# Expert stage of an attention and router kernel: TensorE order given by hand, x eviction ahead of the weight copies, four buffers for the second weight

## Chip, cores and metric

The kernel runs on one core of one Trainium2 chip. The metric is the device time of one launch in microseconds (us), the median of several runs; lower is better. In what follows PE is TensorE, PEld its weight loads, ACT is ScalarE, DVE is VectorE, POOL is GpSimd and SP is SyncE.

## What is computed

Attention with polynomial sketch features, and behind it a layer of eight experts. A router gives each of 4352 tokens (128 numbers each) to one expert, by the best cosine. All is float32. Cut to what matters here:

```python
x = attention_output.reshape(4352, 128)          # N tokens of D = 128
expert_idx = np.argmax(logits, axis=1)           # one of E = 8 experts for each token
for e in range(8):
    mask = expert_idx == e
    h = np.maximum(x[mask] @ w1[e], 0.0)         # w1[e]: 128 x 1024
    out[mask] = gate_w[mask, None] * (h @ w2[e]) # w2[e]: 1024 x 128
```

## The kernel before

The first part (up to about 110 us) computes the attention and the logits. Its instructions are recorded in ticks, and a scheduler sets their order on each engine. The tokens, scaled by their gates, are written to a DRAM buffer `x_dram`. Then `route_and_run_experts` sorts the tokens by expert and pads each expert's group to whole blocks of 128 tokens; 41 blocks always suffice (`NBLK`). One integer per block, `exp_i`, says whose expert's block it is.

The experts run one block at a time. Both weights of all experts lie in SBUF (`w1_sb`, `w2_sb`). For a block i there are these steps:

- `fetch(i)` (L494 on): POOL issues an indirect DMA that gathers the 128 tokens of the block from `x_dram` into `xs` (L497). Fetches are recorded four blocks ahead (`AHEAD`); `xs` has six buffers.
- `prepare(i)` (L501 to L512): DVE loads the expert's number into a register, copies that expert's first weight to `w1b` (L506) and the second to `w2b` (L507); both tags, `kp` and `a`, have two buffers, shared with the attention part. PE transposes `xs` into PSUM (L510), and DVE evicts the result to `xTb` (L512).
- `up(i)` (L514 to L522): eight matmuls in two halves of four (u = 0 and 1), each half into its own half of a PSUM tile `ps_big` of 2 x 512 columns (L521). Behind each half, ACT applies relu and writes that half of `hT` (L522). `ps_big` and `hT` have two buffers.
- `down(i)` (L524 to L533): eight matmuls add up into `ps_acc` (L528), ACT copies the sum to `y` (L530), and POOL issues an indirect DMA that scatters `y` to the rows of the output (L531).

In each pass of the loop the recording order is fetch of block i + 4, `up(i)`, `prepare(i + 1)`, `down(i - 1)`.

What sets the order on the engines: the whole of `route_and_run_experts` is recorded with `tc.manual_schedule` for DVE alone. So DVE runs its instructions as recorded, while PE, ACT, POOL and SP get theirs from the scheduler. The scheduler mixes the matmuls of neighbouring blocks: in the built program a typical stretch of PE is half 0 of up, three matmuls of down, a transpose, half 1 of up, one matmul of down, half 0 of the next up. Waits between engines are semaphores that the tile framework sets from the tiles that each instruction reads and writes; a wait holds up all that stands behind it on its engine.

Of the kernel before, what the change touches and what calls it, by code (L numbers as in the profile page):

```python
# [11 lines left out]
F32 = mybir.dt.float32  # L12
# [7 lines left out]
P = 128  # L20
B, H, S, D = 4, 4, 1088, 32
R = 8                   # rows of each sketch; R * R features per head
DM = H * D              # 128, the width of a token
N = B * S
E, F = 8, 1024
NF = F // P
HALF = P // 2           # partitions per batch: a tile of tokens is half of two batches
NC = S // HALF          # 17 tiles per pair of batches
NK = S // P             # 8 tiles of keys in each batch by itself, and a 17th of both's rest
SK = NK * P  # L30
NM = B // 2             # pairs of batches
NT = NM * NC            # 34 tiles of 128 tokens
NBLK = (N + E * (P - 1)) // P   # 41: the most blocks of 128 that 8 padded groups of N tokens can fill
K_GROUPS = ((0, 4), (4, 8), (8, 12), (12, 16), (16, 17))
# [3 lines left out]
PROB_EPS = 1e-9  # L38
NOWHERE = 8192.0        # added to a padding slot's destination row: past the output's end
DIGIT = 128             # tokens are counted in two digits  # L40
AHEAD = 4               # blocks whose tokens are fetched ahead of their arithmetic


def bview(t, free):
    """The tile t with the free dims given as [step, count] pairs."""
    return bass.AP(tensor=t.tensor, offset=t.offset, ap=[list(t.ap[0])] + [list(d) for d in free])
# [3 lines left out]
def kernel(  # L50
# [13 lines left out]
    nc = tc.nc  # L64
# [4 lines left out]
    rows_p = ctx.enter_context(tc.tile_pool(name="rows", bufs=4))  # L69
# [11 lines left out]

# [1 line left out]
    swords = consts.tile([2 * R, D, 2], U32, name="swords")  # L83
# [6 lines left out]
    def load_q(m):  # L90
        # token 2*S*m + NC*p + c is row p of tile (m, c)
        for i in range(2):
            for h in range(H):
                nc.sync.dma_start(  # L94
                    q_sb[m][i * HALF:(i + 1) * HALF, :, h],
                    bass.AP(tensor=q.tensor, offset=q.offset + ((2 * m + i) * H + h) * S * D,
                            ap=[[NC * D, HALF], [D, NC], [1, D]]))

    # tiles i * NK + j of keys and values: rows NK*p + j of batch 2*m + i; the last: the rest of both
    v_sb = [consts.tile([P, 6, NC, D], F32, name=f"v{m}") for m in range(NM)]  # L100

# [44 lines left out]

# [1 line left out]
    ident = consts.tile([P, P], F32, name="ident")  # L148
# [13 lines left out]

    # The sketches come as the words of float64 numbers. Float32's sign, exponent and high 23 bits of
    # the mantissa are the same bits, closer together; the low 29 are worth rem * 2**(exponent - 52).
    lo, hi = swords[:, :, 0], swords[:, :, 1]
# [24 lines left out]
    nc.vector.tensor_copy(ST, ps[:, :2 * R])  # L190
    # Sblk and enT are filled up to 96 columns with zeros: wide moving operands for the tensor engine
    Sblk = consts.tile([P, 6, 2 * R], F32, name="Sblk")
# [58 lines left out]

# [1 line left out]
    kz = {}  # L253
    acc = {}

    def k_steps(m, c0, c1):
        n = c1 - c0
        s = {}
# [21 lines left out]
        def kv():  # L280
            if c0 == 0:
                acc[m] = [ps_acc(i)[:, :6 * D].rearrange("p (a n) -> p a n", a=2) for i in range(2)]
            for c in range(c0, c1):
                rest = c == NC - 1
                for i in range(2) if rest else (c // NK,):
                    r = slice(i * HALF, (i + 1) * HALF) if rest else slice(0, P)
                    for p in range(2):
                        nc.tensor.matmul(  # L288
                            acc[m][i][:, p],
                            s["kp"][r, c - c0, 2 * p:2 * p + 2].rearrange("s h i j -> s (h i j)"),  # L290
                            v_sb[m][r, 3 * p:3 * p + 3, c],
                            start=c == i * NK and p == 0, stop=rest, skip_group_check=True)
            if c1 == NC:
                for i in range(2):
                    # per head: its D value columns, then the sum of its features
                    z = consts.tile([P, 2, 2, D + 1], F32, name=f"kz{2 * m + i}")
                    t = acc[m][i]
                    nc.vector.tensor_mul(z[:, :, :, :D], t[:, :, :2 * D].rearrange("p a (h d) -> p a h d", h=2),
                                         bview(maskh, [[0, 2], [1, 2], [0, D]]))
                    zs = t[:, :, 2 * D:2 * D + 1]  # L300
                    nc.vector.tensor_mul(z[:, :, :, D], bview(zs, [list(zs.ap[1]), [0, 2]]),
                                         bview(maskh, [[0, 2], [1, 2]]))
                    kz[2 * m + i] = z.rearrange("p a h d -> p a (h d)")
# [75 lines left out]
    def pick(m):  # L379
        """The first best expert of each token, one-hot."""  # L380
        l, o = lg[:, m], oh[:, m]
# [6 lines left out]
        nc.vector.reduce_max(out=mx[:], in_=t[:], axis=AX.X)  # L388
        # a token with no best one (not a number) goes to the first, as with argmax
        nc.vector.tensor_scalar(t[:, :, 0], mx, 0.0, float(E), op0=ALU.is_equal, op1=ALU.mult)  # L390
# [3 lines left out]
    def gate_tokens(m):  # L394
        """The tokens scaled by their gates and kept in DRAM by token: a positive factor of a token
        is one of its expert's output, which is made of products and relu."""
        l = lg[:, m]
# [15 lines left out]
    def route_and_run_experts():  # L413
# [1 line left out]
        pick(1)  # L415
# [34 lines left out]

        # token + 1 of each slot of each block, 0 where the slot is padding: sums of one product each,
        # of its two digits, which like the one-hot factors are whole in bfloat16
        ps_tok = ps_acc(0)[:, :2 * NBLK]
# [28 lines left out]

        # the expert of each block: how many experts end at or before it
        ends = consts.tile([1, NBLK, E], F32, name="ends")
# [6 lines left out]

# [1 line left out]
        xs, xT, wt, hT = {}, {}, {}, {}  # L493

# [5 lines left out]

        def prepare(i):  # L501
            e = nc.values_load(exp_i[0:1, i:i + 1], engines=(mybir.EngineType.DVE,), min_val=0, max_val=E - 1,
                               skip_runtime_bounds_check_because="a count of experts, clamped to the last one")
            a = work.tile([P, F], F32, tag="kp", name="w1b")
            b = work.tile([P, NF, DM], F32, tag="a", name="w2b")
            nc.vector.tensor_copy(a, w1_sb[:, bass.ds(e, 1)].rearrange("p o f -> p (o f)"))  # L506
            nc.vector.tensor_copy(b, w2_sb[:, bass.ds(e, 1)].rearrange("p o f d -> p (o f) d"))  # L507
            wt[i] = (a, b)
            ps = ps_small()
            nc.tensor.transpose(ps[:, :P], xs.pop(i), ident)  # L510
            xT[i] = work.tile([P, P], F32, tag="sq", name="xTb")
            nc.vector.tensor_copy(xT[i], ps[:, :P])  # L512

        def up(i):  # L514
            ps = ps_big()
            hT[i] = work.tile([P, 2, 512], F32, tag="qp", name="hT")
            x = xT.pop(i)
            for u in range(2):
                for j in range(4):
                    f = 4 * u + j  # L520
                    nc.tensor.matmul(ps[:, u, j * P:(j + 1) * P], wt[i][0][:, f * P:(f + 1) * P], x, start=True, stop=True)  # L521
                nc.scalar.activation(hT[i][:, u], ps[:, u], ACT.Relu)  # L522

        def down(i):  # L524
            ps = ps_acc(i % 2)[:, :DM]
            h, w = hT.pop(i).rearrange("p u n -> p (u n)"), wt.pop(i)[1]
            for f in range(NF):
# [5 lines left out]
                in_=y[:], in_offset=None, bounds_check=N - 1, oob_is_err=False)  # L533

        for i in range(AHEAD):
            fetch(i)
        prepare(0)
        for i in range(NBLK + 1):
            if i + AHEAD < NBLK:
                fetch(i + AHEAD)  # L540
            if i < NBLK:
                up(i)
            if i + 1 < NBLK:
                prepare(i + 1)
            if i > 0:
                down(i - 1)
# [24 lines left out]

    with tc.manual_schedule(engines={mybir.EngineType.DVE}):
        route_and_run_experts()
# [30 lines left out]
```

## Time and profile before

| | us |
|---|---|
| median of 3 runs | 317.56 |
| lowest and highest of them | 317.02, 320.74 |
| profiled execution: span from its first to its last instruction | 315.2 |
| busy in this span: PE, PEld | 261.8, 232.3 |
| busy in this span: DVE, ACT, POOL | 139.9, 93.2, 108.3 |
| mean granted clock of TensorE | 0.926 |
| from 147 to 303 us (156 us): PE, PEld busy | 155.6, 149.9 |
| from 147 to 303 us: DVE, ACT, POOL busy | 61.4, 57.7, 80.7 |

The profile shows one execution. Its own time beyond the span is not recorded on the page; the median of the runs is 2.4 us above the span. The page has one busy row for each engine over 40 equal slices of the span, a row of granted TensorE clock (9 means 90% or more of full speed), and groups of equal instructions with their busy time, the mean of one, and the idle time ahead of them with what ended it. The timeline lists the instructions of an engine in order, merged where equal ones follow each other; "x8" counts records, and a float32 matmul of 128 x 128 leaves two weight loads and two matmul records, a transpose one of each.

### The profile page before, as it was taken

How to read it: one execution, taken by the hardware profiler on the slowest of the kernel's cores; microseconds unless marked ns; L12 is line 12 of the kernel's file. 1: busy time of each engine (PE TensorE's matmuls, PEld its weight loads, DVE VectorE, ACT ScalarE, POOL GpSimd, SP SyncE). 2: the span in 40 equal slices, each digit the busy share in tenths (PEclk: the TensorE clock that was granted, in tenths of full speed). 3: DMA queues.
4: the chain of work that ended last, by engine and by line, in shares of the span. 5: the costliest groups of instructions: out<-in, count | busy, mean ns of one | idle time of the engine just before them, and what ended most of it. 6: DMA issues, size and time to landing. Idle time of an engine off the chain costs nothing.

```text
span 315.2 us, 5574 instructions
## 1 busy us (share of the span) xinstructions
PE 261.8 (83%) x2127; PEld 232.3 (74%) x2127; DVE 139.9 (44%) x345; ACT 93.2 (30%) x236; POOL 108.3 (34%) x103
## 2 busy tenths in 40 slices
PE   1987999999799620319999999999999999999960
PEld 1886777776577410218999999999999999999960
DVE  7234345434654379962444444444444444444300
ACT  1122244224243300002333333333333333333320
POOL 4000000001240233047555555555555555522230
PEclk9998999999999855557999999999999999999996
DMA  6899799990003003002111111101111111200000
GB/s 133 149 136 174 143 177 338 343 322 10 0 2 141 3 0 141 0 17 50 44 34 28 34 30 36 34 29 35 32 33 36 32 35 27 35 16 19 16 2 0
DMA packets 51195, 22.60 MB, mean 72 GB/s; under 512 B 38425, under 2 KB 48676, under 8 KB 50912
## 3 DMA queue, kind: packets, MB, share of 16 engines
q1 hardware_dynamic: 48544, 17.31, 23.8%
q0 software_dynamic: 2624, 4.92, 6.0%
q8 instruction: 17, 0.28, 0.4%
q14 instruction: 10, 0.08, 0.1%
HBM read 17.77 MB, written 4.92 MB: 72 GB/s over the span
## 4 chain that ended last, share of the span: by engine, by line
PE 58%; issue 18%; DVE 9%; SPq 6%; DMA 3%; POOL 2%; ACT 1%; POOLq 0%; DVEq 0%; ACTq 0%
PE ps_big L521 27%; PE ps_acc L528 22%; PE ps_big L328 4%; SPq L94 2%; SPq L104 2%; PE ps_big L348 2%; DVE row L466 2%; PE ps_t L510 1%; DVE qp L340 1%; DVE col L465 1%; DMA emb_sb<-in_moe_expert_emb_dram 1%; DVE upto L434 1%; POOL nrm L399 1%; SPq L111 1%; DMA xs<-x_dram,src_i 1%
## 5 line engine op out<-in xcount | busy, mean ns | idle before, releaser
L521 PE MATMUL ps_big<-xTb,w1b 128*128 128x128 f32 x656 | 93.6, 287 | 0.9 <-issue 0.5
L528 PE MATMUL ps_acc<-w2b,hT 128*128 128x128 f32 x656 | 88.6, 275 | 0.0
L522 ACT ACTIVATE hT<-ps_big 128x512 f32<-128x512 f32 x82 | 49.0, 598 | 126.6 <-PE ps_big L521 110.6
L521 PEld LDWEIGHTS ps_big<-xTb,w1b 128*128 128x128 f32 x656 | 80.9, 194 | 6.9 <-ACT hT L522 4.5
L528 PEld LDWEIGHTS ps_acc<-w2b,hT 128*128 128x128 f32 x656 | 81.3, 192 | 0.1
L497 POOL DMA_INDIRECT xs<-x_dram,src_i x41 | 48.7, 1188 | 55.0 <-PE ps_t L510 32.1
L507 DVE COPY w2b<-w_sb 128x1024 f32 x41 | 28.5, 694 | 84.7 <-PE ps_acc L528 81.3
L531 POOL DMA_INDIRECT out_dram<-y,dst_i x41 | 41.7, 1018 | 41.3 <-ACT hT L522 17.8
L506 DVE COPY w1b<-w_sb 128x1024 f32 x41 | 30.3, 739 | 11.4 <-PE ps_big L521 5.5
L399 POOL TENSOR_TENSOR nrm<-ssq,half_c 128x17 f32<-128x17 f32 x2 | 6.2, 3086 | 65.4 <-ACT sq L367 65.4
L340 DVE TENSOR_TENSOR qp<-a_sb,ps_big 128x768 f32<-128x768 f32 (+1 forms) x10 | 10.6, 1055 | 23.0 <-PE ps_big L328 19.9
L288 PE MATMUL ps_acc<-v,kp 128*128 128x96 f32 (+1 forms) x144 | 19.8, 295 | 0.8 <-DVE kp L276 0.8
L288 PEld LDWEIGHTS ps_acc<-v,kp 128*128 128x128 f32 (+1 forms) x144 | 18.2, 206 | 2.9 <-DVE kp L276 1.6
L469 PE MATMUL ps_acc<-col,row 128*128 128x82 bf16 x34 | 3.0, 269 | 18.3 <-DVE row L466 18.3
L276 DVE TENSOR_TENSOR kp<-ps_t,b_sb 128x256 f32<-128x256 f32 x34 | 12.1, 416 | 13.8 <-ACT b_sb L272 13.8
L367 ACT ACTIVATE sq<-x 128x128 f32<-128x128 f32 x34 | 10.3, 307 | 24.2 <-DVE x L356 24.2
L328 PE MATMUL ps_big<-qT,Sa 128*128 128x384 f32 (+1 forms) x40 | 16.9, 545 | 0.0
L469 PEld LDWEIGHTS <-row 128*128 128x128 bf16 x34 | 2.3, 138 | 19.6 <-DVE row L466 19.6
L328 PE MATMUL ps_big<-qT,Sb 128*128 128x384 f32 (+1 forms) x40 | 16.5, 534 | 0.0
L510 PE MATMUL ps_t<-ident,xs 128*128 128x128 f32 x41 | 11.7, 285 | 5.1 <-DMA xs<-x_dram,src_i 5.1
L270 PE MATMUL ps_t<-Sblk,kT 128*128 128x96 f32 x68 | 12.6, 325 | 1.4 <-ACT kT L265 1.4
L348 PE MATMUL ps_big<-kz,qp 128*64 128x66 f32 x272 | 11.0, 227 | 3.1 <-DVE qp L340 2.9
(137 smaller groups left out, 219.5 us busy)
## 6 DMA issues: line engine op xcount, KB each, us to landing
w_sb<-in_moe_w_dram SPq DMA_DIRECT2D x16, 512.0 KB, 8.1
q<-in_q_dram SPq DMA_DIRECT2D x16, 136.0 KB, 4.1
x_dram<-x SPq DMA_DIRECT2D x2, 1088.0 KB
k<-in_k_dram SPq DMA_DIRECT2D x16, 128.0 KB, 3.8
v<-in_v_dram SPq DMA_DIRECT2D x8, 256.0 KB, 3.3
xs<-x_dram,src_i POOLq DMA_INDIRECT x41, 2.8
out_dram<-y,dst_i POOLq DMA_INDIRECT x41, 2.3
k<-in_k_dram SPq DMA_DIRECT2D x4, 32.0 KB, 3.3
```

Source lines behind the costliest of these rows:

```text
L288: nc.tensor.matmul(acc[m][i][:, p], s["kp"][r, c - c0, 2 * p:2 * p + 2].rearrange("s h i j -> s (h i j)"), v_sb[m][r, 3 * p:3 * p + 3, c], ...
L328: nc.tensor.matmul(ps[:, p, :w], S_[:, 2 * p:2 * p + 2].rearrange("p h i j -> p (h i j)"), s["qT"][:, :w], start=True, stop=True)
L340: nc.vector.tensor_mul(s["qp"][:, :, :w], s["a"][:, :, :w], ps[:, :, :w])
L348: nc.tensor.matmul(ps[i * HALF:(i + 1) * HALF, j, p * W:(p + 1) * W], s["qp"][:, p, j * P + i * HALF:j * P + (i + 1) * HALF], kz[2 * m + i ...
L497: nc.gpsimd.indirect_dma_start(out=xs[i][:], out_offset=None, in_=x_dram[:, :], in_offset=bass.IndirectOffsetOnAxis(ap=src_i[:, i:i + 1], ...
L506: nc.vector.tensor_copy(a, w1_sb[:, bass.ds(e, 1)].rearrange("p o f -> p (o f)"))
L507: nc.vector.tensor_copy(b, w2_sb[:, bass.ds(e, 1)].rearrange("p o f d -> p (o f) d"))
L510: nc.tensor.transpose(ps[:, :P], xs.pop(i), ident)
L521: nc.tensor.matmul(ps[:, u, j * P:(j + 1) * P], wt[i][0][:, f * P:(f + 1) * P], x, start=True, stop=True)
L522: nc.scalar.activation(hT[i][:, u], ps[:, u], ACT.Relu)
L528: nc.tensor.matmul(ps, h[:, f * P:(f + 1) * P], w[:, f], start=f == 0, stop=f == NF - 1)
L531: nc.gpsimd.indirect_dma_start(out=out[:, :], out_offset=bass.IndirectOffsetOnAxis(ap=dst_i[:, i:i + 1], axis=0), in_=y[:], in_offset=None ...
```

## The change

- PE joins DVE in the manual schedule: its instructions in this function run in the order in which they are recorded.
- `prepare` is split into `turn` (transpose and its eviction to `xTb`) and `weights` (register load and the two weight copies). In the loop `turn(i + 1)` comes ahead of `weights(i + 1)`; ahead of the loop `weights(0)` comes first.
- `w2b` moves from the tag `a` (two buffers) to the pool of the `rows` tiles, which has four buffers and holds k, q and x in the attention part.

The recording order of a pass is now fetch of block i + 4, `up(i)`, `turn(i + 1)`, `weights(i + 1)`, `down(i - 1)`, and PE keeps it. Comments were taken out too; behind L497 the line numbers differ.

```diff
-        xs, xT, wt, hT = {}, {}, {}, {}
+        xs, xT, w1b, w2b, hT = {}, {}, {}, {}, {}
...
-        def prepare(i):
-            e = nc.values_load(exp_i[0:1, i:i + 1], engines=(mybir.EngineType.DVE,), min_val=0, max_val=E - 1,
-                               skip_runtime_bounds_check_because="a count of experts, clamped to the last one")
-            a = work.tile([P, F], F32, tag="kp", name="w1b")
-            b = work.tile([P, NF, DM], F32, tag="a", name="w2b")
-            nc.vector.tensor_copy(a, w1_sb[:, bass.ds(e, 1)].rearrange("p o f -> p (o f)"))
-            nc.vector.tensor_copy(b, w2_sb[:, bass.ds(e, 1)].rearrange("p o f d -> p (o f) d"))
-            wt[i] = (a, b)
+        def turn(i):
             ps = ps_small()
             nc.tensor.transpose(ps[:, :P], xs.pop(i), ident)
             xT[i] = work.tile([P, P], F32, tag="sq", name="xTb")
             nc.vector.tensor_copy(xT[i], ps[:, :P])
 
+        def weights(i):
+            e = nc.values_load(exp_i[0:1, i:i + 1], engines=(mybir.EngineType.DVE,), min_val=0, max_val=E - 1,
+                               skip_runtime_bounds_check_because="a count of experts, clamped to the last one")
+            w1b[i] = work.tile([P, F], F32, tag="kp", name="w1b")
+            w2b[i] = rows_p.tile([P, NF, DM], F32, tag="rows", name="w2b")
+            nc.vector.tensor_copy(w1b[i], w1_sb[:, bass.ds(e, 1)].rearrange("p o f -> p (o f)"))
+            nc.vector.tensor_copy(w2b[i], w2_sb[:, bass.ds(e, 1)].rearrange("p o f d -> p (o f) d"))
+
...
-            x = xT.pop(i)
+            x, w = xT.pop(i), w1b.pop(i)
...
-                    nc.tensor.matmul(ps[:, u, j * P:(j + 1) * P], wt[i][0][:, f * P:(f + 1) * P], x, start=True, stop=True)
+                    nc.tensor.matmul(ps[:, u, j * P:(j + 1) * P], w[:, f * P:(f + 1) * P], x, start=True, stop=True)
...
-            h, w = hT.pop(i).rearrange("p u n -> p (u n)"), wt.pop(i)[1]
+            h, w = hT.pop(i).rearrange("p u n -> p (u n)"), w2b.pop(i)
...
-        prepare(0)
+        weights(0)
+        turn(0)
         for i in range(NBLK + 1):
             if i + AHEAD < NBLK:
                 fetch(i + AHEAD)
             if i < NBLK:
                 up(i)
             if i + 1 < NBLK:
-                prepare(i + 1)
+                turn(i + 1)
+                weights(i + 1)
             if i > 0:
                 down(i - 1)
...
-    with tc.manual_schedule(engines={mybir.EngineType.DVE}):
+    with tc.manual_schedule(engines={mybir.EngineType.DVE, mybir.EngineType.PE}):
         route_and_run_experts()
```

## The prediction

> **What bounds the kernel now.** I read the page's slices and costliest groups first, to find the stage, and the timeline of the expert stage second, to find what ends its waits.
>
> ```profile
> PE   1987999999799620319999999999999999999960
> PEclk9998999999999855557999999999999999999996
> ...
> L522 ACT ACTIVATE hT<-ps_big 128x512 f32<-128x512 f32 x82 | 49.0, 598 | 126.6 <-PE ps_big L521 110.6
> L521 PEld LDWEIGHTS ps_big<-xTb,w1b 128*128 128x128 f32 x656 | 80.9, 194 | 6.9 <-ACT hT L522 4.5
> ...
> L507 DVE COPY w2b<-w_sb 128x1024 f32 x41 | 28.5, 694 | 84.7 <-PE ps_acc L528 81.3
> ```
>
> From the 19th slice on (142 us) PE is full, from the 20th on (150 us) at full clock, until 303 us: the expert stage is half of the span, and PE sets its length. DVE and ACT idle there, so the 81.3 us for which DVE waited ahead of the w2b copy (L507) lie off the path. The one wait that PE's weight loads show is for ACT: 4.5 us ahead of L521, ended by the relu (L522). The timeline says what this wait is (columns: start, length, engine and operation, count, idle before it and its releaser):
>
> ```profile
> 229.09 0.28 DVE L512 COPY xTb<-ps_t 128x128 f32<-128x128 f32 x1
> 229.29 0.68 DVE L506 COPY w1b<-w_sb 128x1024 f32 x1
> 229.48 0.97 PEld L521 LDWEIGHTS ps_big<-xTb,w1b 128*128 128x128 f32 x8
> ...
> 230.74 0.60 ACT L522 ACTIVATE hT<-ps_big 128x512 f32<-128x512 f32 x1 [2.00 <-PE ps_big L521]
> 231.04 0.14 PEld L510 LDWEIGHTS ps_t<-ident,xs 128*128 128x128 f32 x1
> ...
> 231.39 0.97 PEld L521 LDWEIGHTS ps_big<-xTb,w1b 128*128 128x128 f32 x8 [0.21 <-ACT hT L522]
> ...
> 232.50 0.97 PEld L521 LDWEIGHTS ps_big<-xTb,w1b 128*128 128x128 f32 x8
> ...
> 233.39 0.97 PEld L528 LDWEIGHTS ps_acc<-w2b,hT 128*128 128x128 f32 x8
> ...
> 233.76 0.60 ACT L522 ACTIVATE hT<-ps_big 128x512 f32<-128x512 f32 x1 [0.58 <-PE ps_big L521]
> ...
> 234.41 0.97 PEld L521 LDWEIGHTS ps_big<-xTb,w1b 128*128 128x128 f32 x8
> ```
>
> Each float32 matmul leaves two records and each transpose one. The eight records of 232.50 end where the next begin, at 233.39: 0.89/8 = 0.1115 us a record. A block is 8 up, 8 down and 1 transpose: 33 records, 3.68 us. Two blocks take 7.80 us (the pattern of 226.61 returns at 234.41), so 3.90 each: PE loses only 0.22 us a block.
>
> The rows also show a dependency. A block's up comes in two halves of four matmuls (u = 0, 1), a relu behind each. The first half starts at 229.48, its relu runs 230.74 to 231.34, and the second half starts at 231.39. Again: 232.50, 233.76 to 234.36, 234.41. The distance is 1.91 us both times, of which 0.89 is the first half's issue, 0.37 the way to ACT, 0.60 the relu and 0.05 the way back. The second half thus waits for the relu of the first half of the same block. They use different halves of one tile (`ps_big`), and in both built programs the second half's first matmul carries a wait for exactly that relu. In the kernel before, the scheduler fills these 1.91 us with down and transpose of neighbouring blocks (from 230.37 to 231.15 here, the whole of 233.39 to 234.28 there), so 1.02 us of waiting shrinks to 0.13 to 0.21.
>
> **The change, part by part.**
>
> *PE order by hand.* The built order is, per block: up half 0, up half 1, transpose of the next block, down of the block before. Nothing stands between the halves, so the whole wait shows: 1.91 - 0.89 = 1.02 us, with down and the transpose queued behind it on PE. The new block is 1.91 (half 0 to half 1) + 0.89 (half 1) + 0.11 (transpose) + 16 x 0.1115 = 1.78 (down) = 4.70 us (4.697 unrounded), against 3.90. No other wait is left on PE: down's operands are a block old (the second relu ends 0.97 us behind half 1, before down of that block by more than 3 us).
>
> *x eviction ahead of the weight copies.* It removes a small wait: at 229.48 up started 0.11 us behind the end of the xTb copy (L512), which ran late behind w2b. About 0.09 us every second block was lost there; this is inside the 3.90. What becomes late instead is w1b: the chain is now transpose, xTb, register load, w1b, up, all within transpose and down, 0.11 + 1.78 = 1.90 us. The short end: transpose to xTb 0.42 (0.11 of issue, 0.27 of matmul, 0.04 on), w1b 0.20 behind the start of xTb (229.09 to 229.29), 0.68 copy, 0.05: 1.35. The long end, from the first cold blocks and the longest copy: 0.52 (140.24 to 140.76), 0.28, 0.21 of issue, 0.81, 0.05: 1.87. Both fit, so I take 0, covered by down; without down this would cost about 1.3 us a block, as it does at the start below.
>
> *Four buffers for w2b.* DVE's 81.3 us of waiting go, worth nothing: w2b is needed a block later. The `rows` buffers it takes were last used by the attention stage and by the copy to DRAM at 120.9 us, which the fetches wait for anyway.
>
> *Queues.* POOL has the same 41 fetches and 41 stores, 1.2 + 1.0 + twice 0.3 us of issue = 2.8 us a block, below 4.70. The first store now stands behind nine fetches instead of ten; fetches run four blocks ahead, more with the longer block. SP's order is unchanged. ACT needs 2 x 0.60 + 0.27 us a block.
>
> *The start.* Until about 145.6 us the granted clock is 0.50 (a record 0.223; cut into windows of 1 us, the trace has 0.50 up to 145 and 0.64 from 145 to 146). The first transpose (140.24) and xTb (to 141.05) stay. Half 0 of block 0 goes at 141.1, takes 1.78, then 0.33 + 0.60 + 0.05: half 1 at 143.9. It ends near 145.7; the transpose of block 1 goes behind it. No down exists yet, so the chain above shows: up of block 1 starts 1.3 later, at 147.0. Then 39 blocks of 4.70 lead to up of block 40 at 147.0 + 183.2 = 330.2. Its halves end 1.91 + 0.89 later, 333.0, and two downs take 32 x 0.1115 = 3.57: last issue 336.6. In the kernel before, the last down starts at 302.78 (in the timeline) and ends 16 records later at 304.57. The difference is **+32.0 us**. What follows (y, a store waiting for the store before it, the closing of the queues) keeps its form: 0 to +1 us.
>
> The profiled span is 315.2 us, and the median of the runs 317.56, so 2.4 us lie around it; I leave them there: 347.2 of span, 317.56 + 32.0 = 349.6, and 349.8 with some of the tail.
>
> **The clock.** A busy share that falls could cost more than its gaps. Rows of the attention stage (columns: window, length, PE, PEld, DVE, ACT, POOL, then granted clock, DMA share, GB/s):
>
> ```profile
> 20.00:25.00 5.00, 4.12 (x36) 3.67 (x34) 1.81 (x6) 1.28 (x4) 0.00 (x0) 1.00 1.28 145
> 25.00:30.00 5.00, 3.38 (x30) 3.09 (x30) 2.80 (x15) 0.59 (x3) 0.57 (x1) 0.97 0.91 185
> 30.00:35.00 5.00, 5.00 (x21) 3.77 (x20) 2.06 (x5) 0.85 (x2) 0.00 (x0) 0.69 1.11 211
> ```
>
> Here PEld is 3.67 of 5 us busy, with pauses of 0.66 and 0.67, and the clock stays 1.00; it falls only after a pause of 1.72 us (27.57 to 29.28). The new expert stage has PEld 3.68 of 4.70 busy, 78%, with one pause of 1.02. It lies between these and nearer to the first, so I take full clock. At the start, with pauses of 1.0 and 1.3, the cold phase may last a few microseconds longer: 0 to 2 us.
> The Trainium skill, "TensorE: Matmul & The Clock Gate", section "A second HAM failure mode: psum-queue depth-cycling", speaks against this change: frequent micro-idles between groups of matmuls can make the clock swing between half and full. By the row the sum stays 349.8; if by that page half of the blocks ran at half clock, it would be an estimated 74 us more, some 424.
>
> **The rivals.**
>
> *PE becomes dense, as a hand-given order could make it.* If the second half of up didn't have to wait, up of block 1 would start at 146.0 (141.1 + 3.57 + 1.3), and 39 blocks of 3.68 with 1.78 + 3.57 would end at 294.9: 9.7 us less, 307.9. For it: the 0.22 us a block that PE loses. Against: the distance of 1.91 us, with a start 0.05 behind the relu. 4%.
>
> *The change moves nothing that counts*, PE reaching around the wait to the down behind it: 312 to 322. Against: at 231.18 and 234.28 PE stood still with down queued behind. 2%.
>
> *w1b comes late.* The wait for w1b joins the relu's, if the chain from transpose to up is over 1.90 us. At 0.2 us a block it gives 39 x 0.2 = 8 more: 358. Against: even the long end is 1.87. 5%.
>
> *The clock falls in part of the stage.* At half clock a block is 1.78 + 0.37 + 0.60 + 0.05 + 1.78 + 0.22 + 3.57 = 8.4 us. It decides from one block in ten on (4 x 3.7 = 15 more, 365; a fifth gives 379). Against: the row of 20 to 25 us. 5%.
>
> **How the numbers follow.** Forecast 84%: 349.8, by its own terms (pitch read to 0.02 us, start 0 to 2, tail 0 to 1) 348 to 353. The range reaches to late weights above and, below, to a relu wait 0.1 us a block shorter: 345 to 358. A change of 2% (6.4 us) is about what a measurement of this kernel tells from none: faster 4%, same 2%, slower 94%.
>
> **What would show it.** Right: up's second half always 1.91 us behind its first, with about 1.0 us of PEld idle ended by the relu, some 40 us in all; a block period of 4.70; clock 1.00 from 150 us; hardly any DVE wait for ps_acc ahead of w2b. The forecast is wrong if the halves are 0.89 apart (the dense rival), if up's first half waits for the w1b copy, or if the clock drops behind 150 us.

## Result and profile after

The changed kernel takes 354.4 us (median of 4 runs, 353.1 to 356.0), the kernel before 318.5 beside it: a ratio of 1.112, 95% interval 1.105 to 1.119. It is slower, as forecast, inside the range of 345 to 358; the forecast was 349.8. The profiled execution has a span of 351.3 us against 315.2. From the start of the first transpose (L510, now L503) to the start of the last copy of y, the expert stage takes 200.8 us against 164.7: the whole difference of the spans, 36.1 us, lies in this stage. Behind it 10.2 and 10.3 us follow. Executions more than 1.5% above the fastest one of their kernel (one each of e1, e2, e4 and e7 below) are left out of the ratios, and the profiles of e4 and e7 are of such an execution.

From the page of the changed kernel, the slices and the groups of the expert stage:

```profile
PE   1988999997994011788888888888888888888770
...
PEclk9998999999996555569999999999999999999995
...
L522 PEld LDWEIGHTS ps_big<-xTb,w1b 128*128 128x128 f32 x656 | 83.0, 198 | 41.2 <-ACT hT L523 38.8
...
L523 ACT ACTIVATE hT<-ps_big 128x512 f32<-128x512 f32 x82 | 49.0, 597 | 110.3 <-PE ps_big L522 110.3
...
L513 DVE COPY w2b<-w_sb 128x1024 f32 x41 | 28.5, 695 | 0.0
```

PE is no longer full: eights in place of nines. The idle time ahead of up's weight loads, ended by the relu, grew from 4.5 to 38.8 us, and DVE's wait ahead of the w2b copy went from 84.7 us to nothing. Both came as forecast; only the first one lies on the path. One block in the timeline:

```profile
228.95 0.14 PEld L503 LDWEIGHTS ps_t<-ident,xs 128*128 128x128 f32 x1
...
229.06 1.86 PEld L529 LDWEIGHTS ps_acc<-w2b,hT 128*128 128x128 f32 x16
...
229.37 0.29 DVE L505 COPY xTb<-ps_t 128x128 f32<-128x128 f32 x1 [2.90 <-PE ps_t L503]
...
229.87 0.69 DVE L512 COPY w1b<-w_sb 128x1024 f32 x1 [0.20 <-DVE xTb L505]
...
230.85 0.97 PEld L522 LDWEIGHTS ps_big<-xTb,w1b 128*128 128x128 f32 x8
...
232.11 0.60 ACT L523 ACTIVATE hT<-ps_big 128x512 f32<-128x512 f32 x1 [0.69 <-PE ps_big L522]
232.76 0.97 PEld L522 LDWEIGHTS ps_big<-xTb,w1b 128*128 128x128 f32 x8 [0.94 <-ACT hT L523]
...
233.64 0.14 PEld L503 LDWEIGHTS ps_t<-ident,xs 128*128 128x128 f32 x1
...
235.54 0.97 PEld L522 LDWEIGHTS ps_big<-xTb,w1b 128*128 128x128 f32 x8
```

Half 0 of up starts at 230.85, its relu ends at 232.71, half 1 starts at 232.76: 1.91 us apart. The next block's half 0 comes at 235.54, 4.69 behind. The last record before the wait is longer in the trace than its share of the issue, so the wait is listed as 0.94 rather than 1.02. The w1b copy for the half that starts at 230.85 ends at 230.56, 0.29 us earlier.

### The profile page after: what moved, and what is told of

Read it like the earlier page. It is cut to its first block, busy times and chain, and to the rows that moved or that the text cites. A ratio compares the mean times of both kernels' runs of the same rounds, so it can differ in the third digit from the quotient of the medians.

```text
span 351.3 us, 5555 instructions
## 1 busy us (share of the span) xinstructions
PE 267.1 (76%) x2127; PEld 235.3 (67%) x2127; DVE 140.1 (40%) x345; ACT 93.2 (27%) x236; POOL 103.1 (29%) x103
## 5 line engine op out<-in xcount | busy, mean ns | idle before, releaser
L522 PE MATMUL ps_big<-xTb,w1b 128*128 128x128 f32 x656 | 94.8, 289 | 32.5 <-ACT hT L523 30.8
L522 PEld LDWEIGHTS ps_big<-xTb,w1b 128*128 128x128 f32 x656 | 83.0, 198 | 41.2 <-ACT hT L523 38.8
L529 PE MATMUL ps_acc<-w2b,hT 128*128 128x128 f32 x656 | 81.5, 279 | 0.0
L529 PEld LDWEIGHTS ps_acc<-w2b,hT 128*128 128x128 f32 x656 | 78.1, 195 | 0.0
L497 POOL DMA_INDIRECT xs<-x_dram,src_i x41 | 43.9, 1071 | 74.4 <-PE ps_t L503 52.9
L505 DVE COPY xTb<-ps_t 128x128 f32<-128x128 f32 x41 | 11.9, 291 | 121.8 <-PE ps_t L503 116.7
L512 DVE COPY w1b<-w_sb 128x1024 f32 x41 | 28.4, 694 | 9.2 <-DVE xTb L505 7.9
L531 ACT COPY y<-ps_acc 128x128 f32<-128x128 f32 x41 | 10.9, 265 | 55.1 <-PE ps_acc L529 55.1
L367 ACT ACTIVATE sq<-x 128x128 f32<-128x128 f32 x34 | 10.3, 307 | 24.2 <-DVE x L356 24.2
L503 PE MATMUL ps_t<-ident,xs 128*128 128x128 f32 x41 | 11.6, 284 | 4.2 <-DMA xs<-x_dram,src_i 4.2
```

The source lines that it names most:

```text
L497: nc.gpsimd.indirect_dma_start(out=xs[i][:], out_offset=None, in_=x_dram[:, :], in_offset=bass.IndirectOffsetOnAxis(ap=src_i[:, i:i + 1], ...
L512: nc.vector.tensor_copy(w1b[i], w1_sb[:, bass.ds(e, 1)].rearrange("p o f -> p (o f)"))
L522: nc.tensor.matmul(ps[:, u, j * P:(j + 1) * P], w[:, f * P:(f + 1) * P], x, start=True, stop=True)
L529: nc.tensor.matmul(ps, h[:, f * P:(f + 1) * P], w[:, f], start=f == 0, stop=f == NF - 1)
```

## Experiments

The kernels e1, e3, e4, e6, e7 and e10 start from the changed kernel, e2 and e5 from the kernel before; e8 and e11 build on e1. Ratios are to the kernel before, run on the same chip.

**A PSUM tile for each half of up (e1).**

```diff
-            ps = ps_big()
...
             for u in range(2):
+                ps = psum.tile([P, 512], F32, tag="big", bufs=2, name="ps_half")
                 for j in range(4):
...
-                    nc.tensor.matmul(ps[:, u, j * P:(j + 1) * P], ...
+                    nc.tensor.matmul(ps[:, j * P:(j + 1) * P], ...
-                nc.scalar.activation(hT[i][:, u], ps[:, u], ACT.Relu)
+                nc.scalar.activation(hT[i][:, u], ps, ACT.Relu)
```

> The changed kernel, but each half of up gets a PSUM tile of its own (one bank, tag big) in place of half of a common tile; the order by hand stays. Theory (the second half of up waits for the relu of the first half only because both lie in one tile, and the hand-given order leaves that wait bare): the halves follow each other at 0.89 us in place of 1.91, a block takes 33 x 0.1115 = 3.68 us in place of 4.70, and the time falls by 39 x 1.02 = 40 us and some more at the start, to 311 to 314 us, below the kernel before. Rival (PE's half-to-half distance comes from PE itself, from the relu output tile, or from the clock): the distance stays 1.9 and the time 350 to 355.

Measured: 309.3 us, ratio 0.972 (0.964 to 0.980). Its timeline:

```profile
156.44 1.87 PEld L522 LDWEIGHTS ps_half<-xTb,w1b 128*128 128x128 f32 x16
...
157.71 0.60 ACT L523 ACTIVATE hT<-ps_half 128x512 f32<-128x512 f32 x1 [0.69 <-PE ps_half L522]
158.23 0.15 PEld L503 LDWEIGHTS ps_t<-ident,xs 128*128 128x128 f32 x1
158.34 1.86 PEld L529 LDWEIGHTS ps_acc<-w2b,hT 128*128 128x128 f32 x16
...
160.13 1.87 PEld L522 LDWEIGHTS ps_half<-xTb,w1b 128*128 128x128 f32 x16
```

Both halves now go in one run of 16 records, the relu of the first one beside the second, and a block takes 3.69 us. The order by hand, the eviction and the buffers are those of the changed kernel; the tile alone turned its loss of 36 us into a gain of 9. The relu, its output tile `hT` and PE's order are unchanged, so the rivals named above are out: the cause of the loss is the wait on the common tile, laid bare by the order.

**The order by hand alone, on the kernel before (e2).**

```diff
-    with tc.manual_schedule(engines={mybir.EngineType.DVE}):
+    with tc.manual_schedule(engines={mybir.EngineType.DVE, mybir.EngineType.PE}):
```

> The kernel before with one edit: PE joins the manual schedule. The weight copies stay ahead of the transpose's eviction on DVE, and w2b keeps two buffers. Theory: the bare relu wait comes as in the changed kernel (4.70 us a block), and on top the w2b copy waits for the down of the block before last on PE, which stands behind the transpose, so that xTb is late: 0.31 from the end of down to the copy, 0.62 copy, 0.28 xTb, 0.11 to up = 1.3 us more a block: 6.0 us a block, about 354 + 39 x 1.3 = 405 us. So the other two parts of the change are worth some 50 us once the order is given by hand. Rival (those two parts are worth nothing also under the hand-given order): 354 us.

Measured: 433.8 us, ratio 1.360 (1.346 to 1.374), even slower than expected. Two blocks of it, in the timeline and as windows from up to up (granted clock, DMA share and GB/s last):

```profile
255.47 0.69 DVE L507 COPY w2b<-w_sb 128x1024 f32 x1 [4.51 <-PE ps_acc L528]
...
256.08 0.28 DVE L512 COPY xTb<-ps_t 128x128 f32<-128x128 f32 x1
...
256.48 0.97 PEld L521 LDWEIGHTS ps_big<-xTb,w1b 128*128 128x128 f32 x8 [1.24 <-issue]
...
258.38 1.75 PEld L521 LDWEIGHTS ps_big<-xTb,w1b 128*128 128x128 f32 x8 [0.94 <-ACT hT L522]
```

```profile
250.47:256.48 6.01, 4.18 (x33) 3.83 (x34) 1.50 (x4) 1.46 (x3) 2.04 (x3) 1.00 0.05 16
256.48:264.12 7.64, 5.81 (x33) 5.46 (x34) 1.50 (x4) 1.46 (x3) 2.04 (x3) 0.78 0.06 17
264.12:270.12 6.00, 4.18 (x33) 3.83 (x33) 1.49 (x4) 1.46 (x3) 2.03 (x3) 1.00 0.09 25
```

The mechanism is the expected one: w2b waits for down, xTb for w2b, up for xTb, a second pause of 1.24 us, and a block of 6.0 us. What was not expected is the second line: with pauses of 1.24 and 0.94 us in each block the clock falls to half for a stretch, and such a block takes 7.64 us. In this profile 18 blocks take about 7.6 us and 19 about 6.0, nearly in turn; 18 x 1.63 = 29 us is the gap between 405 and 434. So the early eviction and the four buffers together are worth 79 us under the order by hand, though they are worth nothing under the scheduler's order (e4 below).

**w2b back to two buffers (e3).**

```diff
-            w2b[i] = rows_p.tile([P, NF, DM], F32, tag="rows", name="w2b")
+            w2b[i] = work.tile([P, NF, DM], F32, tag="a", name="w2b")
```

> The changed kernel with w2b back in the tag that has two buffers; order by hand and early eviction stay. Theory: w2b then waits for down, but stands last on DVE and is needed a block later, so nothing is lost: 353 to 355 us, block 4.70. Rival (four buffers are needed as soon as PE's order is fixed): xTb of the next block is held up on DVE behind the waiting w2b copy, and the block grows towards 6.0 us, 400 us.

Measured: 354.3 us, ratio 1.110 (1.101 to 1.119). The profile has the w2b copy waiting again for down, 0.60 us a block, last on DVE:

```profile
228.64 0.97 PEld L522 LDWEIGHTS ps_big<-xTb,w1b 128*128 128x128 f32 x8
...
228.95 0.69 DVE L513 COPY w2b<-w_sb 128x1024 f32 x1 [0.60 <-PE ps_acc L529]
```

Nobody waits for it in that block. The four buffers are worth nothing once the eviction goes first: the early eviction alone undoes the extra loss of e2. Whether four buffers alone would have undone it too, no run shows.

**The scheduler orders PE again (e4).**

```diff
-    with tc.manual_schedule(engines={mybir.EngineType.DVE, mybir.EngineType.PE}):
+    with tc.manual_schedule(engines={mybir.EngineType.DVE}):
```

> The changed kernel with DVE alone in the manual schedule, so that the scheduler orders PE again; early eviction and four buffers stay. The built order of a block is half 0, transpose, three matmuls of down, half 1, five of down. Theory (the loss is all in the hand-given order): 0.11 + 3 x 0.223 = 0.78 us stand between the halves, 0.24 of the 1.02 us is left, block 1.91 + 0.89 + 1.11 = 3.91 us as before: 316 to 320 us. Rival (early eviction or the buffers cost time): over 325 us.

Measured: 318.2 us, ratio 0.999 (0.995 to 1.003). PE's weight loads in one block:

```profile
228.96 0.97 PEld L522 LDWEIGHTS ps_big<-xTb,w1b 128*128 128x128 f32 x8
...
229.85 0.14 PEld L503 LDWEIGHTS ps_t<-ident,xs 128*128 128x128 f32 x1
...
229.96 0.75 PEld L529 LDWEIGHTS ps_acc<-w2b,hT 128*128 128x128 f32 x6
...
230.87 0.97 PEld L522 LDWEIGHTS ps_big<-xTb,w1b 128*128 128x128 f32 x8 [0.16 <-ACT hT L523]
...
232.87 0.97 PEld L522 LDWEIGHTS ps_big<-xTb,w1b 128*128 128x128 f32 x8
```

The halves are again 1.91 apart, with a transpose and three matmuls between them, and a block takes 3.91 us as before. The other two parts together change nothing by themselves: all of the loss belongs to the order, with the common tile kept.

**The split tile in the kernel before (e5).** The edit is that of e1.

> The kernel before with the PSUM tile of up split in two, the scheduler ordering PE. The built order of a block is half 0, half 1, three matmuls of down, transpose, five of down, first half of the next up. Theory (the tile's wait also costs the kernel before its 0.13 to 0.21 us a block): no relu wait is left, but xTb still stands behind w2b on DVE, which waits for down: down ends 0.67 behind half 1, then 0.31 + 0.62 + 0.28 + 0.11 to the next up, 2.0 us, against 1.9 us of PE work: 3.8 us a block, 314 us. Rival (the wait was fully hidden before): 318 us.

Measured: 312.6 us, ratio 0.980 (0.974 to 0.987).

```profile
203.28 0.69 DVE L507 COPY w2b<-w_sb 128x1024 f32 x1 [2.28 <-PE ps_acc L528]
...
203.89 0.28 DVE L512 COPY xTb<-ps_t 128x128 f32<-128x128 f32 x1
...
204.29 1.86 PEld L521 LDWEIGHTS ps_half<-xTb,w1b 128*128 128x128 f32 x16
```

The up before it started at 200.52, so a block takes 3.77 us. The kernel before is faster by 1.3 to 2.6% without the common tile, so the wait cost it as well. What is left is the late xTb behind w2b: up starts 0.12 behind its end. So DVE's wait for down, which the prediction put off the path, limits the block once the tile is split.

**Another order by hand, common tile kept (e6).**

```diff
             if i < NBLK:
-                up(i)
+                up(i, 0)
             if i + 1 < NBLK:
                 turn(i + 1)
                 weights(i + 1)
             if i > 0:
-                down(i - 1)
+                down(i - 1, 0)
+            if i < NBLK:
+                up(i, 1)
+            if i > 0:
+                down(i - 1, 1)
```

Here `up(i, u)` is one half, and `down(i, u)` four of the eight matmuls.

> The changed kernel with another order by hand and the common tile kept: half 0 of up, transpose of the next block, first half of down, half 1 of up, second half of down. Theory (the wait is harmless if 1.02 us of other PE work stand in it): transpose and four matmuls of down are 1.0 us, the halves stay 1.91 us apart, a block takes 1.91 + 0.89 + 0.89 = 3.70 us, 311 to 313 us, equal to the split tile. Rival (order by hand itself is slow on PE): over 318 us.

Measured: 310.4 us, ratio 0.971 (0.965 to 0.977). PE's weight loads:

```profile
203.79 0.97 PEld L526 LDWEIGHTS ps_big<-xTb,w1b 128*128 128x128 f32 x8
204.68 0.97 PEld L535 LDWEIGHTS ps_acc<-w2b,hT 128*128 128x128 f32 x8
205.57 0.97 PEld L526 LDWEIGHTS ps_big<-xTb,w1b 128*128 128x128 f32 x8
206.47 0.14 PEld L503 LDWEIGHTS ps_t<-ident,xs 128*128 128x128 f32 x1
206.58 0.97 PEld L535 LDWEIGHTS ps_acc<-w2b,hT 128*128 128x128 f32 x8
207.49 0.97 PEld L526 LDWEIGHTS ps_big<-xTb,w1b 128*128 128x128 f32 x8
```

Half 0 at 205.57, half 1 at 207.49: 1.92, with 1.00 us of other work in between and about 0.02 us lost. From one half 1 (203.79) to the next (207.49) a block takes 3.70 us. An order by hand isn't slow as such. The dependency may stay if its length is filled.

**The clock at the start (e7 and e10).** The prediction put up of block 2 at about 151.7 us (147.0 + 4.70); it came at 155.5. In windows of the changed kernel:

```profile
142.00:144.00 2.00, 1.31 (x7) 1.02 (x6) 0.00 (x0) 0.60 (x1) 1.52 (x2) 0.50 0.27 66
...
146.00:148.00 2.00, 0.71 (x3) 0.51 (x3) 1.55 (x3) 0.60 (x1) 1.27 (x2) 0.50 0.14 33
...
154.00:156.00 2.00, 2.00 (x12) 2.00 (x11) 0.38 (x1) 0.01 (x1) 0.00 (x0) 0.51 0.12 33
156.00:158.00 2.00, 1.25 (x11) 1.06 (x11) 0.00 (x0) 0.85 (x2) 1.02 (x1) 1.00 0.00 0
```

The weight loads of these blocks show the pauses. Behind them stand one line of the kernel before, then two lines and two windows of e1:

```profile
143.91 1.78 PEld L522 LDWEIGHTS ps_big<-xTb,w1b 128*128 128x128 f32 x8 [0.98 <-ACT hT L523]
...
147.49 1.78 PEld L522 LDWEIGHTS ps_big<-xTb,w1b 128*128 128x128 f32 x8 [1.69 <-DVE w1b L512]
150.25 1.78 PEld L522 LDWEIGHTS ps_big<-xTb,w1b 128*128 128x128 f32 x8 [0.98 <-ACT hT L523]
```

```profile
144.42 2.47 PEld L521 LDWEIGHTS ps_big<-xTb,w1b 128*128 128x128 f32 x16 [0.87 <-issue]
```

```profile
143.66 0.14 PEld L503 LDWEIGHTS ps_t<-ident,xs 128*128 128x128 f32 x1
145.40 1.86 PEld L522 LDWEIGHTS ps_half<-xTb,w1b 128*128 128x128 f32 x16 [1.59 <-issue]
```

```profile
142.00:144.00 2.00, 2.00 (x12) 1.81 (x10) 0.00 (x0) 0.62 (x2) 1.48 (x2) 0.62 0.19 47
144.00:146.00 2.00, 0.61 (x6) 0.60 (x6) 1.59 (x3) 0.57 (x1) 1.70 (x2) 1.00 0.26 51
```

The granted clock stays at 0.50 until late in the first long unbroken stretch (150.3 to 156), while e1, whose first 3.3 us of up have no pause, had it at 1.00 from 144 us. The other profiles agree. The clock is back 3.9 to 7.4 us behind the first transpose in the kernel before, e1, e4, e5 and e6, which have at most one pause between their first up and that moment. It is back 12.2 to 15.7 us behind it in the changed kernel, e2, e3 and e7, whose first two blocks have three pauses of 0.8 to 1.7 us. To test it, matmuls that nobody reads were added where PE waits ahead of the stage:

```diff
+WARM = (4, 4, 4, 9)
...
+            idle = ps_small()
+            for j in range(WARM[t0 // 9]):
+                nc.tensor.matmul(idle[:, :P], ones, before, start=True, stop=True)
```

> The changed kernel with 21 matmuls added on PE between and behind the groups that find the tokens of each slot (4, 4, 4 and 9, results read by nobody), where PE otherwise waits for DVE and the first fetch. Theory (the miss of 4 us against the prediction is the half clock, which lasted to 156 us in place of 146): the clock is 1.00 when block 0 starts, up of block 2 starts near 150 in place of 155.5, and the time falls by 5 us to 349; the block stays 4.70. Rival (the miss lies elsewhere, or the pauses of the first blocks drop the clock again): 353 to 355 us.

Measured: 354.7 us, ratio 1.108 (1.100 to 1.117): no gain. The clock rose to 1.00 at about 142 us of that execution and was back at 0.50 from 148.5 us on, where a pause of 2.34 us ahead of the first transpose ends. This did not decide the question, so the last group was lengthened to 19 (e10).

> The changed kernel with 4, 4, 4 and 19 added matmuls (before: 4, 4, 4 and 9, where the clock rose to 1.00 and fell again in the pause of 2.3 us ahead of the first transpose). The last group now reaches up to that transpose: 19 x 0.223 = 4.2 us. Theory (the miss of 4 us is the half clock at the start): block 0 starts at full clock, from the first transpose to up of block 2 it takes 10 us in place of 15.2, and the time is 349 us. Rival (the pauses of blocks 0 and 1, 1.0 and 1.4 us in a row, drop the clock again): 353 to 355 us.

Measured: 352.0 us, ratio 1.099 (1.090 to 1.108). In the profile:

```profile
146.00:148.00 2.00, 1.27 (x9) 1.03 (x9) 0.29 (x1) 0.75 (x2) 1.39 (x3) 1.00 0.18 43
148.00:150.00 2.00, 1.16 (x8) 0.97 (x8) 1.31 (x2) 0.04 (x2) 1.70 (x2) 1.00 0.30 57
150.00:155.00 5.00, 4.38 (x24) 4.38 (x25) 1.60 (x3) 1.17 (x2) 2.17 (x3) 0.66 0.15 37
```

Block 0 and the first half of block 1 ran at full clock. Behind the pauses of block 1 (1.53 and 0.88 us) the clock fell to 0.50 for one more stretch of about 3.4 us. So theory and rival each hold in part. From the first transpose to up of block 2 it took 11.4 us (143.66 to 155.04) in place of 15.25, and the stage 196.8 in place of 200.8. That is the 4 us that the prediction missed (its own terms make the stage 336.6 + 0.36 - 140.24 = 196.7). The timed runs are less clear on it: 352.0 against 354.4 with overlapping intervals, since the attention part ahead of the stage varies by more than that from run to run (the first transpose stood at 140.3 and 143.7 us in these two profiles).

**All of it together (e8 and e11).** The split tile, the added matmuls, and `turn(i + 1)` and `weights(i + 1)` recorded between the halves of up, with 9 (e8) or 19 (e11) matmuls in the last group.

> The split tile in the changed kernel, the same 21 added matmuls, and the transpose and weight copies of the next block recorded between the halves of up, so that block 1 does not wait for its weights. Theory: from 141.1 us on 1352 records of 0.1115 us, with 0.5 of pause behind block 0, to 292.3 us against 304.6 in the kernel before: 12 us less, 306 us. Rival (the clock is still half at block 0): 2 to 3 us more, 308 to 309.

> The split tile, the transpose and weight copies between the halves of up, and 4, 4, 4 and 19 added matmuls. Theory: no long pause is left once the stage begins, so the clock stays at 1.00 and block 0 saves about 2 us against the version with 9: 304 us. Rival (the clock falls in the pause ahead of block 0 also here, or the added matmuls delay the first transpose): 306 us or more.

Measured: 306.2 us (e8), ratio 0.961 (0.954 to 0.968), and 307.3 us (e11), ratio 0.963 (0.957 to 0.970). Both stages take 154 us (154.0 and 153.8), against 155.2 in e1. So about one microsecond came from the start, and the two can't be told apart; e11's 304 was not reached. In e8 the clock was at 0.50 in block 0; in e11 it was at 1.00 there, but PE's weight loads then paused for 0.8 us between 150 and 152 us. Nearly all of the gain over the kernel before is the tile and the dense order.

## Why the prediction was right, and where it was off

*The dependency of the halves* held to the hundredth: 1.91 us from half to half, 38.8 us of idle weight loads ended by the relu ("some 40" forecast), block 4.69 against 4.70. That the wait comes from the common tile, and not from PE or the relu's output, was argued from the two halves' use of one tile and from the wait in the built programs; e1 shows it, as its edit changes the tile alone, and e6 shows that the same wait costs nothing once it is filled.

*The other parts at nothing*: right for the changed kernel. With the order left to the scheduler they change nothing (e4), and w2b's buffers nothing under the order by hand once the eviction goes first (e3). The prediction named down as the cover of the chain from transpose to up; in e2, where xTb stands behind w2b and so behind down, the end of the chain shows: up waits 1.24 us a block. In the changed kernel the chain took 1.61 us from the start of the transpose (228.95) to the end of the w1b copy (230.56), 1.66 with the 0.05 of the way back, inside the 1.35 to 1.87 given. The short end had one term too small: w1b starts 0.50 us behind the start of xTb, not 0.20.

*The start* is the term that was mis-sized. "The cold phase may last a few microseconds longer: 0 to 2 us" was the row, and 0 went into the sum; it cost 3.8. About 0.4 of this is the chain ahead of up of block 1: the sum had 1.3 us, worked out at full clock, and the pause was 1.69 (147.49 in place of 147.0). The other 3.4 are block 1 itself, 8.05 us from up to up (147.49 to 155.54) in place of 4.70; the prediction's own price of a block at half clock was 8.4. So the step that failed is the clock's return at 145.6. It was taken from the kernel before, whose first block has one pause of 0.87 us and then runs on without another until the clock is back. The changed kernel's first two blocks have three pauses of 1.0 to 1.7 us (0.98, 1.69 and 0.98), and the clock stayed at half until about 156. That these pauses held it there is what the profiles and e10 point to; what exactly decides the moment of the return is not shown, and with the same order it came 13.5 (e3) to 15.7 us behind the first transpose. By its own terms the forecast allowed 348 to 353; the measured 354.4 lies above that. It is inside the outer range partly by luck, as that range had its upper reach for late weights and not for the clock at the start. The remaining 0.3 of the stage's 36.1 us is about one relu late in the stage, at 326.27, that started 1.54 behind its up in place of 1.26; its cause is not known.

*The dense rival* failed as stated, but its price was nearly right: e1, which gives it its condition, took 309.3 where 307.9 stood, and its stage 155.2 where the rival's terms make 294.9 + 0.36 - 140.24 = 155.0. *The clock rival* did not come in the changed kernel, where PEld is busy 78% of a block with one pause of 1.02 us: 1.00 from 156 us to the end of the stage. It came in e2, with 64% (3.83 of 6.01) and two pauses.

The Trainium skill, "TensorE: Matmul & The Clock Gate", section "A second HAM failure mode: psum-queue depth-cycling", was weighed with 424 us. For the changed kernel the row won; in e2 the swing between half and full clock that the page describes was seen (1.00 in a block of 6.01 us, 0.78 in the next of 7.64).

The same page, section "Why this matters for your kernels", advises no PE pauses above some 3 us. The runs here go against taking that as a safe bound: e2's clock fell with no pause longer than 1.24 us, and e10's behind pauses of 1.53 and 0.88.

## What to carry to other kernels

Before giving an engine's order by hand, look for instructions that start just behind another engine's end (here 0.05 us behind the relu, at the same distance each time): these are dependencies that the scheduler has been filling, and a tidy order lays them bare, once per pass. Two halves of one tile may count as one thing to the waits, as they do here. Separate tiles for what is written and read at different times (e1, ratio 0.972) and an order that fills the wait (e6, 0.971) do equally well here. Edits that are worth nothing on the old order can be what the new one needs, so try each part alone and against the whole.

## What was not expected of the hardware

In these profiles the longest pause of TensorE alone does not decide its clock. One pause of 1.02 us in every 4.70 us kept 1.00 for 180 us, and e1 stayed at 1.00 through a single pause of 1.59 us ahead of its block 1 (the prediction's rows have a fall behind one of 1.72). Two pauses of 1.24 and 0.94 us in every 6.0 us (e2) made the clock fall in about every other block, and such a block took 7.64 us. In the first blocks of the changed kernel, pauses of 1.0 to 1.7 us went with a clock of 0.50 for 15 us. This fits a clock that depends on how much of a few microseconds is paused: at 1.00 throughout, the weight loads were busy 78% of a block in the changed kernel and 73% in the prediction's row of 20 to 25 us; in e2 it was 64%. Where the limit lies, and over what time it counts, no run shows.
